# An attention and expert-layer kernel on one core: list scatters in pairs, gathers spread over the units, stored weights in longer runs

## The chip, the core and the metric

The kernel runs on one core of a Trainium2 chip. The metric is the device time of one execution in microseconds (us). Its engines are TensorE (PE, the matmuls; PEld is the loading of its weights), VectorE (DVE), ScalarE (ACT), GpSimd (POOL) and SyncE (SP), which mostly issues transfers. Each works through its own queue in order, and they wait for each other by semaphores.

## What is computed

Attention without softmax, followed by a layer of eight experts of which every token uses at most one:

```python
# 8 batches, 2496 rows, u and v 256 wide, z 64 wide
scores = np.matmul(z, z.transpose(0, 2, 1)) / S
attn = np.maximum(scores, 0.0) ** 2
x = (u * np.matmul(attn, v)).reshape(19968, 256)

out = x.copy()
xc = x[x @ w_skip > 0]                   # the others stay as they are
e_idx = np.argmax(xc @ w_gate, axis=1)   # one of 8 experts
gate_w = softmax of xc @ w_gate, at e_idx
for e in range(8):
    h = np.maximum(xc[e_idx == e] @ w1[e], 0.0)     # 256 -> 1024
    y[e_idx == e] = gate_w[...] * (h @ w2[e])       # 1024 -> 256
out[do_compute] = xc + y
```

All of it is fp32. The kernel splits every operand in a high part and a low part (`ah`/`al`, `vh`/`vl`, `zh`/`zl`, `hh`/`hl`) and multiplies high with high, high with low and low with high.

## The kernel before

**Attention.** A batch has five chunks of queries: four of 512 and a short one of 448, so 40 chunks. A chunk is done in ten steps; a step takes 256 keys. `weights` makes a step's two key tiles: six score matmuls into PSUM (L251), relu and square on ACT (L297, L298), the high part by a cast (`high`, ACT at L304 or DVE at L306, as `on_act` says), the low part by a subtraction on DVE (`low`, L309). Then 24 matmuls (L333) add the step's product with `v` to four accumulators. `stage` prepares a step two steps (`LA`) ahead of its matmuls. At a chunk's last step `part` reads the accumulators (L361, L363), `mul` multiplies by `u` (L366), and later `turn_rows` (L370) and `store` (L379) write the rows to the buffer `xr` in DRAM and to `out`.

The scores are symmetric. For the pairs (chunk c, key block j) in `PAIRS`, chunk c stores its squared scores, transposed (`keep`, L268), and chunk j reads them back instead of computing them (`recall`, L287). The stores are put into a list; `put_some` (L663) issues at most four of them per step, on SP, not before the second step after. `ahead` issues the reads five steps ahead. Where the key block is the short chunk's (j = 4), a pair of key tiles is stored in 14 transfers of 64 KB, of 32 elements (128 bytes) in a run; else in 4 of 256 KB with runs of 128 elements (512 bytes). The short chunk recalls four of its ten steps, 4 to 7, and casts (ACT) and subtracts (DVE) 2 × 448 = 896 columns in one operation each.

**Routing.** After every second chunk, `routing` works out to which expert each of about 1000 tokens goes: `gates` two steps later, `logits` three, `route` and `counts` four, and `place` six. `place` has eight small matmuls, five small DVE operations (L472 to L477) that end in `dest`, the slot of each token in its expert's list, and eight indirect transfers on POOL (L480), each of which scatters the 8-byte entries of 128 tokens into `lst` in DRAM. The order of all this is the order of the code: `after` and `todo` say at which step each function runs, and the instructions stand in the engines' queues as the functions issue them. The last routing runs in the first unit of expert 0 (`end_routes`); the one before it, after chunk 38, in steps of chunk 39.

**Experts.** An expert's list is worked through in units of two tiles of 128 tokens. Three units (`NFIX`) are always done; a switch then picks an arm with as many further tiles as the list has (units of two or three). Before a unit its rows must be gathered (`fetch`, L528, one indirect transfer on POOL per tile), transposed on PE (`turn_pe`, L546) and split (ACT L548, DVE L549). The unit itself is 48 matmuls for the hidden layer (L575), relu and split (L580, L581), 48 matmuls back (L594), the combination (L623) and two scatters of the results (L624) on POOL. `fills` says which side work is issued after which part of a unit, by slot numbers 0 to 7: gathers, transposes, and the pieces of the next expert's weights (`load_w`), whose low parts POOL subtracts (L151 and L157, for the experts from 2 on).

Rows sit in tiles `xgf` (four: two per parity of the expert, its first two units) and `xgu` (four, in turn). In the fixed unit i of an expert after the first, slot 0 gathers unit i + 2, and in unit 0 slot 1 gathers the next expert's units 0 and 1 together (`next_rows`). An arm gathers two units ahead where there are so many.

## Time and profile before

| | us |
|---|---|
| runs | 1937.83, 1925.1, 1917.16; median 1925.1 |
| profiled execution | 1936.81, its span 1935.0 |
| mean granted clock of TensorE | 0.983 of full speed |
| busy: PE, DVE, ACT, POOL | 1836.9, 1212.5, 1107.0, 418.9 |
| list scatters (L480) | 160, 1.134 each |
| gathers (L528) | 84, about 1.03 each |
| recalled short chunk tiles | 32 casts of 0.938, 32 subtractions of 1.082 |

Attention fills the span to about 1400 us, and the experts the rest. A window's row gives its length, then the busy time and the number of instructions of each engine in it, then PEclk (the clock that TensorE was granted, as a share of full speed), the share of the DMA engines' time in use and GB/s. A group's row gives the busy time, the mean of one instruction in ns, and behind the bar the idle time before them and what ended it. A row of the timeline gives start, length, engine, line, operation, and in brackets the idle time before and its end; "remote" there means that the record of what ended it is not in the trace.

### The profile page before, as it was taken

What the parts mean: (1) busy time and instruction counts of PE and PEld (TensorE: products, weight loads), DVE (VectorE), ACT (ScalarE), POOL (GpSimd) and SP (SyncE); (2) the same over time, 40 slices, a digit from 0 to 9 for tenths busy, and PEclk for the clock granted to TensorE, in tenths of its full rate; (3) what the DMA queues carried; (4) which work ended last, traced back from release to release, by engine and by line L of the source; (5) the groups of instructions that cost most, each with busy time, mean ns of one, the idle gap of its engine ahead of it and who ended that gap; (6) DMA issues with size and microseconds to landing.
All of it is one profiled execution on the core that took longest, in us unless ns stands there. A gap on an engine that the chain in (4) does not pass through costs nothing.

```text
span 1935.0 us, 40227 instructions
## 1 busy us (share of the span) xinstructions
PE 1836.9 (95%) x15928; PEld 1595.0 (82%) x15928; DVE 1212.5 (63%) x1998; ACT 1107.0 (57%) x1350; POOL 418.9 (22%) x417
## 2 busy tenths in 40 slices
PE   8999999899999999999999999999889989999998
PEld 6888778777877877787878788777789989998998
DVE  6777777677777777777777777767643333333333
ACT  8766676667667666756775775666423223322321
POOL 0111110110110111011021011101334345534532
PEclk9999999999999999999999999999989999999999
DMA  5584677377557747775783777468542223212211
GB/s 175 122 172 115 157 185 163 81 192 168 129 123 192 148 101 183 173 155 109 174 172 88 182 173 157 107 144 174 115 112 64 63 85 96 71 56 83 76 36 34
DMA packets 468400, 246.98 MB, mean 128 GB/s; under 512 B 321571, under 2 KB 410917, under 8 KB 468080
## 3 DMA queue, kind: packets, MB, share of 16 engines
q1 hardware_dynamic: 454656, 221.61, 49.4%
q0 software_dynamic: 13136, 21.42, 3.8%
q8 instruction: 142, 2.33, 0.5%
q14 instruction: 178, 1.46, 0.3%
q10 hardware_dynamic: 288, 0.17, 0.0%
HBM read 134.79 MB, written 108.95 MB: 126 GB/s over the span
## 4 chain that ended last, share of the span: by engine, by line
PE 63%; DMA 9%; DVE 8%; ACT 7%; issue 6%; SPq 4%; another core or an unknown queue 2%; POOL 1%; POOLq 0%; DVEq 0%; ACTq 0%
PE acc L333 36%; PE psh L575 9%; PE y L594 9%; PE ps L251 7%; DMA out<-o,idt 4%; ACT r L297 2%; ACT r L298 2%; DVE al L309 2%; SPq L379 2%; ACT ah L304 2%; DMA kept<-rt 2%; SPq L663 1%; DVE rt L268 1%; PE psm L401 1%
## 5 line engine op out<-in xcount | busy, mean ns | idle before, releaser
L333 PE MATMUL acc<-ah,vh 64*128 64x512 f32 (+1 forms) x3120 | 739.3, 391 | 41.0 <-ACT xrow L361 17.8
L333 PE MATMUL acc<-ah,vl 64*128 64x512 f32 (+1 forms) x3120 | 719.9, 389 | 0.2
L309 DVE TENSOR_TENSOR al<-r,ah 128x1024 fp32r<-128x1024 f32 (+1 forms) x400 | 475.7, 1194 | 199.1 <-ACT ah L304 179.6
L333 PE MATMUL acc<-al,vh 64*128 64x512 f32 (+1 forms) x3120 | 566.2, 387 | 2.0 <-DVE al L309 1.2
L333 PEld LDWEIGHTS acc<-ah,vh 64*128 64x128 f32 x3120 | 426.5, 186 | 121.9 <-ACT xrow L361 21.8
L333 PEld LDWEIGHTS acc<-ah,vl 64*128 64x128 f32 x3120 | 427.3, 187 | 49.7 <-issue 2.0
L297 ACT ACTIVATE r<-ps 128x1024 f32<-128x1024 f32 (+1 forms) x292 | 294.4, 1008 | 259.3 <-PE ps L251 178.3
L480 POOL DMA_INDIRECT lst<-pair,dest x160 | 181.4, 1134 | 1180.8 <-DVE dest L477 1119.5
L333 PEld LDWEIGHTS acc<-al,vh 64*128 64x128 f32 x3120 | 364.6, 186 | 58.5 <-DVE al L309 6.0
L298 ACT ACTIVATE r<-r 128x1024 f32<-128x1024 f32 (+1 forms) x292 | 304.6, 1043 | 9.2
L304 ACT CAST ah<-r 128x1024 fp32r<-128x1024 f32 (+1 forms) x265 | 271.5, 1036 | 32.9 <-DMA r<-kept 13.6
L580 ACT ACTIVATE hh<-psh 128x512 fp32r<-128x512 f32 (+1 forms) x172 | 99.6, 585 | 316.2 <-PE psh L575 251.1
L594 PE MATMUL y<-w2t,hh 128*128 128x256 f32 x1328 | 249.9, 289 | 0.8 <-issue 0.8
L575 PE MATMUL psh<-xt,w1h 128*128 128x256 f32 (+1 forms) x1280 | 234.5, 286 | 14.4 <-issue 10.2
L581 DVE SCALAR_TENSOR_TENSOR hl<-psh,hh 128x512 fp32r<-128x512 f32 (+1 forms) x172 | 113.8, 672 | 164.4 <-ACT hh L580 138.7
L575 PEld LDWEIGHTS psh<-xt,w1h 128*128 128x128 f32 x1280 | 199.3, 191 | 16.0 <-issue 11.4
L594 PEld LDWEIGHTS y<-w2t,hh 128*128 128x128 f32 x1328 | 210.9, 195 | 1.7 <-issue 1.7
L594 PE MATMUL y<-w2t,hl 128*128 128x256 f32 x664 | 190.0, 286 | 1.8 <-issue 1.8
L575 PE MATMUL psh<-xt,w1l 128*128 128x256 f32 (+1 forms) x640 | 182.1, 285 | 0.0
L251 PE MATMUL ps<-zh 64*128 64x512 f32 (+1 forms) x584 | 145.3, 407 | 14.7 <-ACT r L297 6.8
L306 DVE CAST ah<-r 128x1024 fp32r<-128x1024 f32 (+1 forms) x135 | 90.3, 669 | 86.6 <-ACT r L298 73.3
L251 PE MATMUL ps<-zl,zh 64*128 64x512 f32 (+1 forms) x584 | 141.3, 393 | 0.0
(169 smaller groups left out, 1725.2 us busy)
## 6 DMA issues: line engine op xcount, KB each, us to landing
kept<-rt SPq DMA_DIRECT2D x152, 256.0 KB
r<-kept SPq DMA_DIRECT2D x304, 128.0 KB
raw<-in_v SPq DMA_DIRECT2D x80, 256.0 KB
ut<-in_uT SPq DMA_DIRECT2D x32, 512.0 KB
xr<-xrow SPq DMA_DIRECT2D x128, 128.0 KB
out<-xrow SPq DMA_DIRECT2D x128, 128.0 KB
raw<-in_w SPq DMA_DIRECT2D x64, 256.0 KB
kept<-rt SPq DMA_DIRECT2D x224, 64.0 KB
```

Of the source, the lines that this page charges most:

```text
L251: nc.tensor.matmul(to, k[h, o : o + P], queries(q, h, n), start=(m == 0), stop=(m == 2))
L297: nc.scalar.activation(r[:, :, :n], ps[:, :, :n], AF.Relu, scale=isc)
L298: nc.scalar.activation(r[:, :, :n], r[:, :, :n], AF.Square)
L304: nc.scalar.copy(ah[:, :, :n], r[:, :, :n])
L306: nc.vector.tensor_copy(ah[:, :, :n], r[:, :, :n])
L309: nc.vector.tensor_sub(al[:, :, :n], r[:, :, :n], f32(ah[:, :, :n]))
L333: nc.tensor.matmul(acc[t][:, :n], w[h, x, dd], a[h, x, :n], start=(first and t not in halves[:m]), stop=(last and t not in halves[m + 1 :]),)
L480: put = nc.gpsimd.indirect_dma_start(out=lst, out_offset=bass.IndirectOffsetOnAxis(ap=dest[:, t : t + 1], axis=0), in_=pair[:, t, :], in_o ...
L575: nc.tensor.matmul(ps[:, j * W : (j + 1) * W], wt[:, a, o : o + P], x[:, d, :W], start=(m == 0), stop=(m == 5),)
L580: nc.scalar.activation(hh[:, : G * W], ps[:, : G * W], AF.Relu)
L581: nc.vector.scalar_tensor_tensor(hl[:, : G * W], ps[:, : G * W], 0.0, f32(hh[:, : G * W]), op0=ALU.max, op1=ALU.subtract)
L594: nc.tensor.matmul(ys[t], h[:, tt], w2t[f][:, k, :], start=(f == 0 and m == 0 and t % 2 == 0), stop=(f == NF - 1 and m == 2), skip_group_c ...
```

## The change

*The list scatters.* `place` ends with the sums `df`. A new function `put_in(t0, t1)` computes `dest` for the tiles t0 to t1 and issues their scatters. It runs for two tiles at the steps 6, 8, 10 and 12 after the routing's chunk; for the routing after chunk 38 at 6, 7, 8 and 9; and in `end_routes` for all four tiles at once.

*The gathers.* There are six `xgf` tiles, for all three fixed units of two experts, and `xgu` holds the units of the arms. In fixed unit i of an expert e after the first, slot 0 gathers unit i + 3 and slot 3 gathers unit i of expert e + 1. All six tiles of the arm's first three units are thus reserved ahead of the switch: always three, whether or not the arm has them; in the arm, further units are gathered three ahead. That makes 96 gathers of 128 rows rather than 84. Expert 0's units and the loads of the lists' ids are moved accordingly.

*The short chunk's stored weights.* All stores are 4 transfers of 256 KB in runs of 512 bytes, whatever the key block, and all reads take the full 512 columns, so the short chunk's columns come back in another order. The cast and the subtraction undo that in three pieces: for each of the two key tiles 3 × 128 columns, and 64 columns of both together.

```diff
             dst = kept[c, j].rearrange("(m i) k -> i m k", i=32)
             for a in range(4):
-                h = slice(32 * a, 32 * a + 32)
-                if j < NQ - 1:
-                    puts.append((step[0], dst[:, :, a * P : a * P + P], t[h]))
-                else:
-                    for k in range(4 if a < 2 else 3):
-                        o = k * P + 32 * a
-                        puts.append((step[0], dst[:, :, o : o + 32], t[h, :, 32 * k : 32 * k + 32]))
+                puts.append((step[0], dst[:, :, a * P : a * P + P], t[32 * a : 32 * a + 32]))
...
+        views = [[x[:, :, :n] for x in (r, ah, al)]]
+        if old and n < QC:
+            b3 = 3 * P
+            views = [
+                [r.rearrange("p x (a k e) -> p x k a e", a=4, k=4)[:, x, :3]]
+                + [t[:, x, :b3].rearrange("p (k a e) -> p k a e", a=4, k=3) for t in (ah, al)]
+                for x in range(2)
+            ] + [
+                [r.rearrange("p x (a k e) -> p x k a e", a=4, k=4)[:, :, 3, : (n - b3) // 32, :]]
+                + [t[:, :, b3:n].rearrange("p x (a e) -> p x a e", e=32) for t in (ah, al)]
+            ]
         def high():
-            if on_act(ci, p):
-                nc.scalar.copy(ah[:, :, :n], r[:, :, :n])
-            else:
-                nc.vector.tensor_copy(ah[:, :, :n], r[:, :, :n])
+            for r_, h_, _ in views:
+                (nc.scalar.copy if on_act(ci, p) else nc.vector.tensor_copy)(h_, r_)
         def low():
-            nc.vector.tensor_sub(al[:, :, :n], r[:, :, :n], f32(ah[:, :, :n]))
+            for r_, h_, l_ in views:
+                nc.vector.tensor_sub(l_, r_, f32(h_))
...
             nc.vector.tensor_reduce(df, ds_, axis=AX.X, op=ALU.add)
-            nc.vector.tensor_scalar_add(dest[:, :K], df, float(BIG))
-            puts = []
-            for t in range(K):
+            put_sums.append(df)
+        puts, put_sums = [], []
+        def put_in(t0, t1):
+            df = put_sums[0]
+            nc.vector.tensor_scalar_add(dest[:, t0:t1], df[:, t0:t1], float(BIG))
+            for t in range(t0, t1):
                 put = nc.gpsimd.indirect_dma_start(
...
+                    last = ci + 2 > NC - 1
+                    for t in range(0, 4 * len(new), 2):
+                        k = 6 + (t // 2 if last else t)
+                        after.append((lambda put_in=put_in, t=t: put_in(t, t + 2), k))
...
-        return xgs["f"][2 * (e % 2) + i] if e and i < 2 else xgs["u"][i % 4]
+        return xgs["f"][NFIX * (e % 2) + i] if i < NFIX else xgs["u"][i % 4]
...
             if e:
-                add(fills, (0, lambda: fetch(ids_of(e, i + 2), pair(e, i + 2))))
-                add(fills, (3, lambda: turn_pe(pair(e, i + 1), turned(e, i + 1))))
-                if more and i == 0:
-                    add(fills, (1, lambda: next_rows(e + 1)))
-                if more and i == 1:
-                    add(fills, (5, lambda: turn_pe(pair(e + 1, 0), turned(e + 1, 0))))
+                add(fills, (0, rows(e, i + 3)), (3, lambda: turn_pe(pair(e, i + 1), turned(e, i + 1))))
+                if e == 1 and i == 0:
+                    fills[0].insert(0, rows(1, 2))
+                if more:
+                    add(fills, (3, rows(e + 1, i)))
...
+            elif i == 1:
+                add(fills, (3, lambda: turn_pe(pair(0, 2), turned(0, 2))), (5, rows(0, 3)), (5, rows(0, 4)))
...
             else:
-                    add(fills, (0, lambda: next_rows(1)), (4, lambda: turn_pe(pair(0, 3), turned(0, 3))),
-                        (7, lambda: turn_pe(pair(1, 0), turned(1, 0))))
+                add(fills, (0, rows(1, 0)), (4, lambda: turn_pe(pair(0, 3), turned(0, 3))),
+                    (4, rows(0, 5)), (4, rows(1, 1)), (6, lambda: load_ids(idts[2], 2, 2 * NSTAT)))
+            if more and i == 2:
+                add(fills, (7, lambda: turn_pe(pair(e + 1, 0), turned(e + 1, 0))))
...
-                    if len(after) > 1 or after[0] == 3:
-                        m = 2 if len(after) > 1 else 1
-                        add(fills, (0, lambda: fetch(ids_of(e, i + 2, m), pair(e, i + 2), m)))
+                    if i + 3 < end:
+                        add(fills, (0, rows(e, i + 3)))
```

The order on VectorE after the third routing's `place`, in the first chunks of the second batch, before (L309 is `low`, L306 a cast of `high`, L361 to L366 the reading of the accumulators and the multiply):

```order
L474 TENSOR_TENSOR ds__2789<-psm,ds__2789 128x64
L475 TENSOR_TENSOR ds__2789<-ds__2789,hot 128x64
L476 TENSOR_REDUCE df<-ds__2789 128x8
L477 TENSOR_SCALAR dest<-df 128x8
L309 TENSOR_TENSOR al<-r,ah 128x1024
```

and in the changed kernel, whose line numbers are its own (L314 is `low`, L490 `dest`, L310 a cast, L366 to L371 the accumulators and the multiply):

```order
L490 TENSOR_SCALAR dest<-df 128x2
L314 TENSOR_TENSOR al<-r,ah 128x1024
L268 STREAM_TRANSPOSE rt<-r 128x16x32 x2
L310 CAST ah<-r 128x1024
L314 TENSOR_TENSOR al<-r,ah 128x1024
L490 TENSOR_SCALAR dest<-df 128x2
L314 TENSOR_TENSOR al<-r,ah 128x1024
L268 STREAM_TRANSPOSE rt<-r 128x16x32 x2
L366 COPY xrow<-acc 128x512
L368 TENSOR_TENSOR xrow<-acc,xrow 128x512 x2
L314 TENSOR_TENSOR al<-r,ah 128x1024
L371 TENSOR_TENSOR ut<-xrow,ut 128x1024
```

Before, one `dest` of 128 x 8 stands directly behind the reduction. Now the first of four does, the second stands two steps on, and the third follows the last row shown, directly behind the chunk's multiply.

POOL in the fixed units of expert 2, first before, where `idt_142` holds expert 2's ids and `idt_143` expert 3's:

```order
L528 DMA xgu<-xr,idt_142 128x256 x2
L528 DMA xgf<-xr,idt_143 128x256 x4
L151 TENSOR_TENSOR w1l<-raw,w1h 128x512 x3
L624 DMA out<-o,idt_142 19968x256 x2
L528 DMA xgu<-xr,idt_142 128x256 x2
L151 TENSOR_TENSOR w1l<-raw,w1h 128x512
L157 TENSOR_TENSOR w2t<-raw,w2t 128x256 x4
L624 DMA out<-o,idt_142 19968x256 x2
L858 TENSOR_LOAD arm
L528 DMA xgu<-xr,idt_142 128x256 x2
L157 TENSOR_TENSOR w2t<-raw,w2t 128x256 x4
```

and in the changed kernel (L540 gathers, L636 scatters the results):

```order
L540 DMA xgu<-xr,idt_142 128x256 x2
L151 TENSOR_TENSOR w1l<-raw,w1h 128x512
L540 DMA xgf<-xr,idt_143 128x256 x2
L151 TENSOR_TENSOR w1l<-raw,w1h 128x512 x2
L636 DMA out<-o,idt_142 19968x256 x2
L540 DMA xgu<-xr,idt_142 128x256 x2
L151 TENSOR_TENSOR w1l<-raw,w1h 128x512
L540 DMA xgf<-xr,idt_143 128x256 x2
L157 TENSOR_TENSOR w2t<-raw,w2t 128x256 x4
L636 DMA out<-o,idt_142 19968x256 x2
L875 TENSOR_LOAD arm
L540 DMA xgu<-xr,idt_142 128x256 x2
```

Six gathers in a row have become two pairs with a subtraction between them, and each unit has four gathers; the `xgu` rows of a unit are those of the unit three later, no longer two.

SP in the first batch's chunk 2 to 4, before, with the stores of pair (2, 4), whose key block is the short chunk's (`kept_138`):

```order
L663 DMA kept_138<-rt 32x16x32 x8
L287 DMA r<-kept_137 32x2x512 x4
L663 DMA kept_138<-rt 32x16x32 x4
L95 DMA raw<-in_v 128x512
L663 DMA kept_138<-rt 32x16x32 x2
L287 DMA r<-kept_137 32x2x512 x4
```

and in the changed kernel:

```order
L675 DMA kept_138<-rt 32x16x128 x4
L280 DMA r<-kept_137 32x2x512 x4
L95 DMA raw<-in_v 128x512
L280 DMA r<-kept_137 32x2x512 x4
L384 DMA xr<-xrow 32x16x64 x4
```

Fourteen issues between the reads have become four ahead of them.

More of the change, by code (lines that the diff above doesn't have):

```diff
@@ L490, in place @@
                 puts.append(put)
-        return gates, logits, route, counts, place
+        return gates, logits, route, counts, place, put_in
     def count(name, rows64=True):
@@ L764, in attn_moe @@
                 if ci % 2 == 0:
-                    gates, logits, route, counts, place = routing(new)
+                    gates, logits, route, counts, place, put_in = routing(new)
                     after = [(gates, 2), (rows0, 2), (logits, 3), (rows1, 3), (route, 4), (counts, 4),
                              (store, 4), (store, 5), (place, 6)]
+                    last = ci + 2 > NC - 1
+                    for t in range(0, 4 * len(new), 2):
+                        k = 6 + (t // 2 if last else t)
+                        after.append((lambda put_in=put_in, t=t: put_in(t, t + 2), k))
                     new = []
@@ L771, in attn_moe @@
             else:
-                gates, logits, route, counts, place = routing(new, False)
+                gates, logits, route, counts, place, put_in = routing(new, False)
         for f in todo.pop(s, []):
@@ L775, in attn_moe @@
         put_some()
-    row_tiles("f", 4)
+    row_tiles("f", NFIX)
+    row_tiles("u", 4)
     ps_s_own.close()
@@ L821, in add, with rows @@
             fills.setdefault(k, []).append(f)
-    def next_rows(e):
-        for i in range(2):
-            fetch(ids_of(e, i), pair(e, i))
+    def rows(e, i):
+        return lambda: fetch(ids_of(e, i), pair(e, i))
     for e in range(E):
@@ L843, in attn_moe @@
                     (5, store), (5, store), (6, end_routes))
-            else:
-                if i == 1:
-                    add(fills, (3, lambda: turn_pe(pair(0, 2), turned(0, 2))),
-                        (6, lambda: [fetch(ids_of(0, k), pair(0, k)) for k in (3, 4)]))
-                    add(fills, *zip((1, 3, 5), wq[:3]))
-                else:
-                    add(fills, (0, lambda: next_rows(1)), (4, lambda: turn_pe(pair(0, 3), turned(0, 3))),
-                        (7, lambda: turn_pe(pair(1, 0), turned(1, 0))))
-                    add(fills, *zip((1, 2, 3, 5, 6), wq[3:]))
-            if i == (0 if e else 2) and e + 2 < E:
-                add(fills, (6, lambda: load_ids(idts[e + 2], e + 2, 2 * NSTAT)))
+            elif i == 1:
+                add(fills, (3, lambda: turn_pe(pair(0, 2), turned(0, 2))), (5, rows(0, 3)), (5, rows(0, 4)))
+                add(fills, *zip((1, 3, 5), wq[:3]))
+            else:
+                add(fills, (0, rows(1, 0)), (4, lambda: turn_pe(pair(0, 3), turned(0, 3))),
+                    (4, rows(0, 5)), (4, rows(1, 1)), (6, lambda: load_ids(idts[2], 2, 2 * NSTAT)))
+                add(fills, *zip((1, 2, 3, 5, 6), wq[3:]))
+            if more and i == 2:
+                add(fills, (7, lambda: turn_pe(pair(e + 1, 0), turned(e + 1, 0))))
             if i == NFIX - 1:
@@ L873, in attn_moe @@
                     unit(0, 2, ids_of(0, i), [xg[:, 0, :], xg[:, 1, :]], xts[0])
+            end = NFIX + (sum(ws) + 1) // 2
             for j, w in enumerate(ws):
```

12 lines of the change are left out of this document (7 added, 5 removed).

## The prediction, made before the changed kernel ran

> **What bounds the kernel now.** I read the page first, then windows around every run of list scatters, then the waits of TensorE behind the attention.
>
> ```profile
> span 1935.0 us, 40227 instructions
> PE 1836.9 (95%) x15928; PEld 1595.0 (82%) x15928; DVE 1212.5 (63%) x1998; ACT 1107.0 (57%) x1350; POOL 418.9 (22%) x417
> ```
>
> TensorE (PE) is the bound: 1935.0 − 1836.9 = 98.1 us without a matmul in flight. The change removes no matmul, so it can win only two things: part of that idle time, and busy time that was stretched because the granted clock (PEclk) fell. The question is where both sit.
>
> The list scatters (L480) go out in runs of eight in 18 of the 21 places where they are issued. I took three windows about each of these 18 starts: its first 6 us, the next 12 us, and the 18 us before. Columns: length, busy us and instructions per engine, PEclk, DMA share, GB/s. The sum over the 18 first-6-us windows:
>
> ```profile
> sum 108.00, PE 108.00 PEld 95.73 DVE 80.51 ACT 72.05 POOL 87.80; mean PE 6.00 PEld 5.32 DVE 4.47 ACT 4.00 POOL 4.88
> ```
>
> Three of the 18 next-12-us windows, and the sum of the 18:
>
> ```profile
> 347.80:359.80 12.00, 6.71 (x46) 5.17 (x43) 7.64 (x10) 6.63 (x8) 4.03 (x5) 0.82 0.01 0
> ...
> 1039.90:1051.90 12.00, 8.38 (x54) 6.81 (x52) 8.97 (x12) 5.64 (x6) 4.36 (x5) 0.72 0.02 2
> ...
> 1181.60:1193.60 12.00, 10.79 (x75) 7.99 (x75) 7.53 (x10) 5.31 (x7) 4.51 (x5) 0.86 0.74 138
> ...
> sum 216.00, PE 182.53 PEld 140.46 DVE 146.01 ACT 122.60 POOL 78.00; mean PE 10.14 PEld 7.80 DVE 8.11 ACT 6.81 POOL 4.33
> ```
>
> One of the windows before, and the sum of the 18:
>
> ```profile
> 323.80:341.80 18.00, 17.62 (x195) 16.56 (x193) 14.46 (x39) 9.57 (x13) 0.00 (x0) 1.00 0.68 176
> sum 324.00, PE 314.70 PEld 255.73 DVE 258.06 ACT 221.95 POOL 0.14; mean PE 17.48 PEld 14.21 DVE 14.34 ACT 12.33 POOL 0.01
> ```
>
> The 12 us from the start of two runs of only four scatters:
>
> ```profile
> 73.70:85.70 12.00, 12.00 (x105) 10.69 (x103) 8.82 (x11) 10.00 (x12) 5.08 (x4) 1.00 0.72 167
> 1414.40:1426.40 12.00, 12.00 (x104) 12.00 (x103) 6.00 (x14) 3.89 (x7) 6.95 (x8) 1.00 0.61 96
> ```
>
> While scatters one to four go out nothing happens (108.00 of 108.00); from about the fifth on TensorE loses 216.00 − 182.53 = 33.5 us. In the quiet windows it loses 9.3 in 324, which would be 6.2 in 216, so 27.3 us belong to the scatters. The clock falls in 7 of the 18 windows, to between 0.72 and 0.86; summing (1 − PEclk) × 12 over them gives 15.4 us more. Two runs of four cost nothing: 12.00 of 12.00 each. The worst place, as a timeline:
>
> ```profile
> 341.82 1.17 POOL L480 DMA_INDIRECT lst<-pair,dest  x1 [49.77 <-DVE dest L477]
> ...
> 351.60 0.97 POOL L480 DMA_INDIRECT lst<-pair,dest  x1 [0.30 <-issue]
> 353.63 1.02 ACT L297 ACTIVATE r<-ps 128x1024 f32<-128x1024 f32 x1 [4.73 <-remote]
> 353.73 0.62 DVE L361 COPY xrow<-acc 128x448 f32<-128x448 f32 x1 [2.67 <-remote]
> 356.22 0.80 PE L333 MATMUL acc<-ah,vh 64*128 64x512 f32 x2 [4.97 <-ACT xrow L361]
> ```
>
> These are the first and the eighth scatter on GpSimd (POOL), then ScalarE (ACT) and VectorE (DVE), which had waited 4.73 and 2.67 us for a signal that the trace doesn't hold ("remote") and start again 1.1 us after the eighth scatter's end, and TensorE after them. Transfers hardly ran there (0.01 in row 347.80), so crowded DMA engines are not the cause; a backlog of scatters fits, since runs of four make no gap.
>
> In the expert part, one row of TensorE's waits (us in all, times, longest) and three windows:
>
> ```profile
> PE pst L546 <- DMA xgu<-xr,idt: 11.9, 6, 2.7
> 1564.00:1578.00 14.00, 9.12 (x62) 8.78 (x62) 2.30 (x5) 1.04 (x3) 7.74 (x9) 0.88 0.42 138
> 1757.00:1773.00 16.00, 11.49 (x64) 11.14 (x63) 3.03 (x6) 2.13 (x6) 7.98 (x10) 0.79 0.42 122
> 1818.00:1830.00 12.00, 9.32 (x67) 9.14 (x66) 2.04 (x5) 1.66 (x4) 7.29 (x10) 0.86 0.19 55
> ```
>
> and on the timeline:
>
> ```profile
> 1501.27 1.05 POOL L528 DMA_INDIRECT xgu<-xr,idt  x1 [0.30 <-issue]
> 1504.24 0.41 PE L546 MATMUL pst<-ident,xgu 128*128 128x128 f32 x2 [1.99 <-DMA xgu<-xr,idt]
> ```
>
> TensorE waits 11.9 us, in six places, for gathered rows that it is about to transpose: POOL issues them at 1501.27, TensorE has them at 1504.24. The clock loss beside such waits is 14 × 0.12 + 16 × 0.21 + 12 × 0.14 = 6.7 us. The rest of TensorE's idle time in this part, at the switches between units, is not touched.
>
> **Part A, scatters two at a time.** Each routing now issues two scatters at its steps 6, 8, 10 and 12 (a step is 30 matmuls, at the 12.00 / 105 = 0.114 us of row 73.70 that is 3.4 us), so a pair has some 7 us to itself.
>
> ```profile
> L477 DVE TENSOR_SCALAR dest<-df 128x8 int32<-128x8 f32 x19 | 3.3, 172 | 0.6
> L480 POOL DMA_INDIRECT lst<-pair,dest x160 | 181.4, 1134 | 1180.8 <-DVE dest L477 1119.5 <-issue 41.8 <-DVE cnt L498 18.9
> ```
>
> Added: three small `dest` operations for each of 18 full routings and one more for the four-tile one, 55 × 0.172 = 9.5 us of VectorE in all, half a microsecond in any one chunk. VectorE is busy 14.46 of 18 us at the densest place shown; the work that hides it is the matmuls of two steps lookahead. Without that cover it would cost 9.5 us. Only POOL waits for `dest`, and behind the scatters on POOL there is one small memset for the next routing; nothing else is queued there during attention. At step 10 `dest` stands behind the chunk's multiply, that is after the accumulators have been read, so no accumulator is released later. A pair occupies POOL for 2 × (1.134 + 0.30) = 2.9 us of its 7, so the backlog that takes five scatters to build is never reached. To be won: at most 27.3 + 15.4 = 42.7 us, at least nothing if pairs meet a cost of their own (rivals). I take 36, about 85%: residue of 0.35 us per routing. The last routing has its four pairs one step apart, which is close to the run of eight that it had; I give it nothing either way.
>
> [...] The row first: 1181.60:1193.60 shows 0.86 although it lost only 12.00 − 10.79 = 1.2 us in all. [...]
>
> **Part B, gathers a unit ahead.** In the fixed units of an expert (three units of 96 matmuls, at the 12.00 / 104 = 0.115 us of row 1414.40 that is 11.1 us each, 33.2 us) POOL had ten gathers and six scatters and now has twelve and six, always three tiles of two: the last may be rows that the expert's arm never uses, twelve gathers more in all.
>
> ```profile
> L528 POOL DMA_INDIRECT xgu<-xr,idt x50 | 51.6, 1032 | 50.8 <-issue 25.6 <-DMA xgu<-xr,idt 9.9 <-DVE xt L549 8.2
> L157 POOL TENSOR_TENSOR w2t<-raw,w2t 128x256 fp32r<-128x256 f32 x48 | 33.8, 737 | 0.1
> L151 POOL TENSOR_TENSOR w1l<-raw,w1h 128x512 fp32r<-128x512 f32 x24 | 30.6, 1298 | 0.4
> ```
>
> POOL's bill for these units: 18 × (1.03 + 0.30 before the next, as at 1501.27) = 23.9, the scatters of the results priced like gathers, plus 4 × 1.298 + 8 × 0.737 = 11.1, together 35.0 against 33.2 us. It ends 1.8 us late and catches up in the arm, which has 22 us and no weights. A gather is now due two units after its issue, so 1.8 us of lateness is covered; without that cover it would be 7 × 1.8 = 13 us. All six waits should go, with their clock: 11.9 + 6.7 = 18.6; I take 16. Expert 0's third unit gains between 0 and 10 us from a shorter run of POOL transfers:
>
> ```profile
> 1423.00:1450.00 27.00, 21.80 (x154) 20.40 (x153) 9.73 (x21) 7.35 (x18) 12.23 (x13) 0.81 0.63 161
> ```
>
> (27.00 − 21.80 + 0.19 × 27 = 10.3). The run is still ten long, so I take 0 and keep 10 for the low end.
>
> **Part C, the short chunk's weights.** They leave in 64 stores of 256 KB and not 224 of 64 KB, and are read back at full width. The cast and the subtraction behind them (32 of each) go in three pieces of 384, 384 and 128 columns.
>
> ```profile
> kept<-rt SPq DMA_DIRECT2D x224, 64.0 KB
> ...
> L304 ACT CAST ah<-r 128x896 fp32r<-128x896 f32 x32 | 29.7, 938 | 13.0 <-PE acc L333 9.5 <-DVE al L309 3.5
> L119 ACT CAST vh<-raw 128x512 fp32r<-128x512 f32 x80 | 49.3, 616 | 17.4 <-DMA raw<-in_v 17.2
> L156 ACT CAST w2t<-raw 128x256 fp32r<-128x256 f32 x64 | 22.8, 407 | 11.0 <-DMA raw<-in_w 9.2 <-issue 1.8
> L309 DVE TENSOR_TENSOR al<-r,ah 128x896 fp32r<-128x896 f32 x80 | 86.3, 1082 | 5.7 <-ACT ah L304 0.6 <-DVE ah L306 0.5 <-DMA xr<-xrow 0.3
> L549 DVE TENSOR_TENSOR xt<-pst,xt 128x512 fp32r<-128x512 f32 x38 | 25.9, 683 | 11.9 <-ACT xt L548 8.9 <-issue 2.9
> L549 DVE TENSOR_TENSOR xt<-pst,xt 128x256 fp32r<-128x256 f32 x10 | 4.2, 424 | 29.6 <-ACT xt L548 29.6
> ```
>
> On the line through 256 and 512 columns, ACT needs 2 × 0.51 + 0.30 = 1.32 us for 0.94 (+0.39), DVE 2 × 0.55 + 0.29 = 1.40 for 1.08 (+0.32): 12.4 and 10.1 us over the kernel, in four successive steps of eight short chunks. Window 323.80:341.80 is such a chunk: ACT has 8.4 us free of 18 and DVE 3.5, against 1.6 and 1.3 added. I count 0; uncovered it is 22.5 us. The 160 DMA issues fewer on SP (SyncE), and transfers in longer runs, were waited for by nobody in the rows above: also 0, a few us of gain at best.
>
> **Sum.** 36 + 16 + 0 = 52 us off the profiled execution, 1936.8 → 1885. That run was the slowest of three, 11.7 us above their median; what varies between runs is likely these very waits, so for the median I take half of that off the gain: 1925.1 − 46 = **1879**.
>
> **Rivals.** *The number of scatters matters, not their run.* Then A gives nothing and B stands: 1925 − 16 = 1909. For it: they still number 160, beside the same engines. Against: the four-scatter rows without a gap. [...]
>
> *Only a part is won:* A brings a third or a half of its 42.7 (14 to 21, that is 15 to 22 less than the 36), because gaps move with the step-10 pair to the change of chunks, or B brings half since POOL stays full (8 less). Both together leave 46 − 23 = 23: about 1902.
>
> *Slower: every start of a run has its price.* If the gap is the landing of the last scatter of a group and not the backlog, 27.3 / 18 = 1.5 us come at the end of each of 72 groups rather than of 18: 72 × 1.5 = 109, less 42.7 and 16, is +50, about 1975. It decides from (42.7 + 16) / 72 = 0.8 us for each pair, and is over 1% from 1.1. Against: the runs of four, also with an end, without a gap.
>
> *No effect:* gaps come from where step 6 lies in the chunk and POOL stays saturated: 1925.
>
> **Chances.** Forecast 0.60; part 0.15; only B 0.13; no effect 0.04; slower 0.08. The measurement tells about 1% from no change, 19 us. Faster by more: 0.60 + 0.15 = 0.75. Within: 0.13 + 0.04 = 0.17. Slower: 0.08. Range: down to 1925 − 42.7 − 18.6, with a part of the 10 of expert 0, about 1858; up past B alone, 1912. That leaves out slower, no effect, and edges, some 0.2.
>
> **What would show it.** In the windows of 12 us behind each routing's step 6: TensorE at 11.5 or more, PEclk 1.00, and pairs of scatters 7 us apart. No row `pst` waiting for `xgu` over 1 us. Short-chunk casts as three operations of about 0.5, 0.5 and 0.3 us, with no new wait for them by TensorE. It is wrong if gaps with "remote" stand behind pairs, if ACT or DVE becomes what `acc` matmuls wait for in the short chunk, or if POOL's gathers slip past their unit.

## The result, and the profile after

The changed kernel takes 1863.96 us (median of 4 runs, 1862.88 to 1865.33) where the kernel before takes 1927.63 (4 runs, 1917.16 to 1937.83): a ratio of 0.967, 95% interval 0.9616 to 0.9724. That is 64 us, where 46 were forecast; 1864 lies in the range of 1858 to 1912. On another chip, below, the same two kernels stand much closer.

The top of the page after:

```profile
span 1863.6 us, 40331 instructions
## 1 busy us (share of the span) xinstructions
PE 1803.3 (97%) x15928; PEld 1589.9 (85%) x15928; DVE 1218.0 (65%) x2120; ACT 1113.3 (60%) x1414; POOL 438.3 (24%) x429
```

The matmuls are the same 15928, and still PE's busy time fell by 33.6 us: the same work ran at a higher clock (0.983 of full speed on average before, 0.995 after) and closer together. To see where the 71.4 us between the two profiled spans came from, I cut both at the last attention matmul. Windows of the kernel before:

```profile
0.00:1394.60 1394.60, 1335.44 (x11825) 1097.80 (x11825) 1020.83 (x1648) 951.75 (x1042) 187.31 (x179) 0.99 0.65 150
1394.60:1935.00 540.40, 501.42 (x4103) 497.19 (x4103) 191.71 (x350) 155.25 (x308) 231.56 (x239) 0.97 0.25 70
```

and of the kernel after:

```profile
0.00:1349.00 1349.00, 1308.76 (x11825) 1098.15 (x11825) 1027.05 (x1769) 958.28 (x1107) 192.50 (x177) 1.00 0.63 158
1349.00:1863.60 514.60, 494.52 (x4103) 491.76 (x4103) 190.95 (x351) 154.99 (x308) 245.83 (x252) 0.98 0.28 76
```

Attention gave 1394.6 − 1349.0 = 45.6 us: 18.9 of idle time (59.2 to 40.2) and 26.7 of busy time. The clock's own records, summed over attention, account for 17.1 of the 26.7 (17.1 lost before, nothing after). The experts gave 540.4 − 514.6 = 25.8 us, 18.9 of them idle time.

Behind the routings, the 12 us windows that the prediction used, now after: the fourth and the sixteenth routing, and the sum of the 18.

```profile
341.90:353.90 12.00, 11.77 (x105) 9.75 (x103) 11.30 (x17) 9.16 (x10) 5.19 (x5) 1.00 0.01 2
...
1145.80:1157.80 12.00, 12.00 (x118) 10.76 (x116) 8.72 (x12) 6.84 (x9) 3.20 (x4) 1.00 0.31 91
...
sum 216.00, PE 209.75 PEld 177.49 DVE 180.17 ACT 146.90 POOL 79.51; mean PE 11.65 PEld 9.86 DVE 10.01 ACT 8.16 POOL 4.42
```

6.25 us are lost in 216, where 33.5 were; that is what the quiet windows of before lost (9.3 in 324, which is 6.2 in 216). PEclk is 1.00 in all 18. At the worst place of before, the timeline after reads:

```profile
340.77 1.33 POOL L492 DMA_INDIRECT lst<-pair,dest  x1 [2.00 <-DVE dest L490]
...
342.26 1.03 ACT L290 ACTIVATE r<-ps 128x1024 f32<-128x1024 f32 x1 [0.50 <-PE ps L251]
342.41 1.75 POOL L492 DMA_INDIRECT lst<-pair,dest  x1 [0.30 <-issue]
343.32 1.06 ACT L291 ACTIVATE r<-r 128x1024 f32<-128x1024 f32 x1
343.83 0.62 DVE L366 COPY xrow<-acc 128x448 f32<-128x448 f32 x1
```

Beside the second pair ScalarE waits 0.50 us for a matmul with a name, and no longer 4.73 for "remote".

TensorE's waits in the expert part, first before (three rows), then after:

```profile
PE pst L546 <- DMA xgu<-xr,idt: 11.9, 6, 2.7
PE psh L575 <- issue: 10.2, 5, 2.4
PE psh L575 <- DVE xt L549: 4.2, 1, 4.2
```

```profile
PE y L606 <- issue: 3.6, 5, 1.1
PE pst L558 <- issue: 3.0, 4, 1.1
PE psh L587 <- issue: 2.6, 2, 2.1
PE psh L587 <- DVE xt L561: 1.7, 1, 1.7
```

No wait for gathered rows is left, and 7.6 us of the "issue" wait ahead of the hidden layer went too.

The pieces of the short chunk, and the small `dest`, as groups after:

```profile
L314 DVE TENSOR_TENSOR al<-r,ah 128x384 fp32r<-128x384 f32 x64 | 32.2, 544 | 0.2
L310 ACT CAST ah<-r 128x384 fp32r<-128x384 f32 x64 | 29.5, 509 | 11.1 <-PE acc L338 9.7 <-issue 1.4
L490 DVE TENSOR_SCALAR dest<-df 128x2 int32<-128x2 f32 x78 | 12.5, 160 | 0.7
L310 ACT CAST ah<-r 128x128 fp32r<-128x128 f32 x32 | 9.4, 295 | 0.0
L314 DVE TENSOR_TENSOR al<-r,ah 128x128 fp32r<-128x128 f32 x32 | 9.2, 286 | 0.0
```

### The profile page after: what moved, and what is told of

It is laid out like the page before. It is cut to its first block, busy times and chain, and to the rows that moved or that the text cites. A ratio compares the mean times of both kernels' runs of the same rounds, so it can differ in the third digit from the quotient of the medians.

```text
span 1863.6 us, 40331 instructions
## 1 busy us (share of the span) xinstructions
PE 1803.3 (97%) x15928; PEld 1589.9 (85%) x15928; DVE 1218.0 (65%) x2120; ACT 1113.3 (60%) x1414; POOL 438.3 (24%) x429
## 3 DMA queue, kind: packets, MB, share of 16 engines
q8 instruction: 143, 2.34, 0.6%
## 4 chain that ended last, share of the span: by engine, by line
PE 70%; DVE 9%; ACT 7%; DMA 6%; issue 4%; SPq 3%; POOL 0%; DVEq 0%; POOLq 0%; ACTq 0%
PE acc L338 38%; PE y L606 11%; PE psh L587 11%; PE ps L251 7%; DVE al L314 2%; ACT r L290 2%; ACT ah L310 2%; ACT r L291 2%; SPq L384 2%; DMA out<-o,idt 2%; DVE rt L268 1%; DMA r<-kept 1%; DMA kept<-rt 1%; DVE xrow L368 1%; PE psm L406 1%
## 5 line engine op out<-in xcount | busy, mean ns | idle before, releaser
L314 DVE TENSOR_TENSOR al<-r,ah 128x1024 fp32r<-128x1024 f32 (+3 forms) x464 | 480.4, 1050 | 188.3 <-ACT ah L310 173.2
L338 PEld LDWEIGHTS acc<-ah,vh 64*128 64x128 f32 x3120 | 431.7, 185 | 89.4 <-DVE xrow L368 14.5
L338 PEld LDWEIGHTS acc<-ah,vl 64*128 64x128 f32 x3120 | 432.0, 185 | 46.7
L492 POOL DMA_INDIRECT lst<-pair,dest x160 | 189.0, 1181 | 1141.8 <-DVE dest L490 1101.0
L310 ACT CAST ah<-r 128x1024 fp32r<-128x1024 f32 (+1 forms) x329 | 277.3, 872 | 28.2 <-PE acc L338 11.6
L251 PE MATMUL ps<-zh,zl 64*128 64x512 f32 (+1 forms) x584 | 143.2, 390 | 0.0
```

The lines of the kernel that those rows point to most:

```text
L251: nc.tensor.matmul(to, k[h, o : o + P], queries(q, h, n), start=(m == 0), stop=(m == 2))
L310: (nc.scalar.copy if on_act(ci, p) else nc.vector.tensor_copy)(h_, r_)
L314: nc.vector.tensor_sub(l_, r_, f32(h_))
L338: nc.tensor.matmul(acc[t][:, :n], w[h, x, dd], a[h, x, :n], start=(first and t not in halves[:m]), stop=(last and t not in halves[m + 1 :]),)
L492: put = nc.gpsimd.indirect_dma_start(out=lst, out_offset=bass.IndirectOffsetOnAxis(ap=dest[:, t : t + 1], axis=0), in_=pair[:, t, :], in_o ...
```

## The experiments

Theory: a run of scatters holds TensorE up once it is some five long, and the expert part waits for rows that were gathered too late. Rivals: it is the number of scatters, or the end of each group, that costs; and the parts may overlap or hide each other's loss.

The runs fall into four groups, each on a chip of its own. This matters more than expected: the unchanged kernel before takes 1904.2 us on the first of these chips, 1863.7 on the second, 1902.7 on the third and 1866.4 on the fourth, beside 1927.6 in the result's run, whose chip is not known. So kernels are compared only within a chip.

### Each part alone

The scatters alone, the gathers alone and the stores alone are the hunks of the diff, put one at a time into the kernel before. The fourth kernel has the scatters in fours:

```diff
-                    for t in range(0, 4 * len(new), 2):
+                    for t in range(0, 4 * len(new), 4):
                         k = 6 + (t // 2 if last else t)
-                        after.append((lambda put_in=put_in, t=t: put_in(t, t + 2), k))
+                        after.append((lambda put_in=put_in, t=t: put_in(t, t + 4), k))
```

> The kernel before with only the list scatters in pairs. In the two traces the stretch from the first full routing to the last one but one shrank by 46 us (138.4 to 1345.8 before, 138.6 to 1300.0 after). Theory (a run of scatters is what costs): about 46 us faster than before, some 1881, and the windows behind a routing's step 6 without TensorE's gaps. Rival (their number costs): no difference, 1927. Rival (each start of a group costs): slower than before.

> The kernel before with only the gathers moved. From the last routing to the end the two traces differ by 26 us (549.8 and 523.9 us), 19 of them idle time of TensorE. Theory: about 26 us faster, some 1901, with the 11.9 us of waits for gathered rows gone and most of the 10.2 us that stood as issue in front of the hidden layer's matmuls. By the prediction's term it would be 16, some 1911. If the expert part gained only because the attention part no longer ended in scatters, nothing.

> The kernel before with only the short chunk's stored weights changed. After, TensorE waits 7.3 us in 8 places for ScalarE's cast in front of the attention matmuls, before 2.8 in 3 places. Theory: the three-piece cast costs about 4 to 5 us, some 1932. Rival (longer runs of the stores pay for it, or it is hidden, as predicted): 1927 or a few us less.

> The kernel before with the scatters in two runs of four, at steps 6 and 10, instead of one of eight. Theory (a run costs from about the fifth scatter): like the pairs alone, about 1881 to 1885, since the two runs of four in the kernel before showed no gap. Rival (each group's end has a price of 1.5 us): 18 ends more, about 27 us slower than the run of eights is now, 1950. Rival (number): 1927.

Against 1904.2 us of before on this chip:

| | median us | ratio, 95% interval |
|---|---|---|
| scatters in pairs | 1880.3 | 0.9874 (0.9831 to 0.9918) |
| scatters in fours | 1884.8 | 0.9881 (0.9831 to 0.9932) |
| gathers | 1884.7 | 0.9899 (0.9863 to 0.9935) |
| stores | 1895.9 | 0.9963 (0.9935 to 0.9990) |

The 18 windows of 24 us from each routing's first scatter show the attention part by itself (432 − PE is the loss). The kernel with only the gathers moved still has the runs of eight:

```profile
sum 432.00, PE 408.64 PEld 343.95 DVE 319.65 ACT 282.34 POOL 166.11; mean PE 22.70 PEld 19.11 DVE 17.76 ACT 15.69 POOL 9.23
```

in pairs alone:

```profile
sum 432.00, PE 426.35 PEld 376.93 DVE 348.69 ACT 300.06 POOL 172.62; mean PE 23.69 PEld 20.94 DVE 19.37 ACT 16.67 POOL 9.59
```

in fours:

```profile
sum 432.00, PE 423.73 PEld 367.33 DVE 337.77 ACT 295.34 POOL 178.56; mean PE 23.54 PEld 20.41 DVE 18.77 ACT 16.41 POOL 9.92
```

and in eights with the new stores:

```profile
sum 432.00, PE 416.52 PEld 353.71 DVE 327.72 ACT 296.30 POOL 171.88; mean PE 23.14 PEld 19.65 DVE 18.21 ACT 16.46 POOL 9.55
```

Eights lose 23.4 us, fours 8.3, pairs 5.7, with 160 scatters each time. So it is the run's length; the rivals of number and of the group's end fall (fours have twice the ends of eights and lose a third). The pairs gained 24 us and not 46, mainly because this chip's eights cost less. The attention part of these two traces, eights and pairs, differs by 25.8 us (1370.3 and 1344.5), and in the 18 windows eights lose 23.4 us here and 34.2 in the result's run of before:

```profile
sum 432.00, PE 397.84 PEld 326.33 DVE 305.85 ACT 267.42 POOL 165.80; mean PE 22.10 PEld 18.13 DVE 16.99 ACT 14.86 POOL 9.21
```

The gathers alone gained 19.5, somewhat under the 26 expected; their waits for rows are gone in that trace, and stand unchanged at 11.7 us where only the scatters were changed:

```profile
PE pst L553 <- DMA xgu<-xr,idt: 11.7, 6, 3.1
PE psh L582 <- issue: 6.3, 4, 2.0
```

The stores alone were expected to cost 4 to 5 us. They gained 8: that expectation was wrong, and so was its reason, since the wait for ScalarE's cast, 7.3 us after and 2.8 before, is 6.5 us with pairs alone, without any three-piece cast, and only 3.7 with the stores alone:

```profile
PE acc L333 <- ACT ah L304: 6.5, 7, 0.9
...
PE acc L338 <- ACT ah L310: 3.7, 4, 0.9
```

What the stores gained lies behind the routings too, 8 of their windows' 23.4 us, most plainly at the fourth routing, in a short chunk. First eights with the old stores, then with the new:

```profile
338.80:362.80 24.00, 20.53 (x188) 17.97 (x186) 18.39 (x24) 16.85 (x18) 9.14 (x9) 1.00 0.12 38
```

```profile
339.70:363.70 24.00, 23.77 (x215) 22.46 (x213) 21.03 (x28) 18.48 (x20) 10.59 (x9) 1.00 0.13 38
```

Why they soften the runs of eight there isn't settled: it could be the shorter queue of stores, or the pieces' other timing. These were not tried apart.

### What the runs do to TensorE's signals

The traces hold the times of semaphore updates. TensorE's signalling matmuls, 1343 in before and 1330 in the changed kernel, all update one semaphore; the delay below goes from the end of the signalling matmul to the next update of that semaphore, as a median over the 18 routings, by the time since the routing's first scatter. Single values can be wrong where a record is missing, medians less so. The entries move with the edges of the bins: in the first row a shift by half a microsecond takes the one at 2-4 us to 0.40 or 0.71, and the one at 4-6 us, with six matmuls, to 0.80 or 2.06. Worked out from the traces:

```
us since the first scatter     0-2   2-4   4-6   6-8   8-10  10-12 12-14
before (result's run)          0.02  0.60  1.31  2.34  1.55  0.61  0.01
gathers alone (eights)         0.02  0.25  0.76  1.21  0.74  0.79  0.01
stores alone (eights)          0.02  0.13  0.27  0.94  0.22  0.71  0.01
before (third chip)            0.02  0.04  0.63  0.57  0.02  0.77  0.01
fours alone                    0.02  0.13  0.72  0.01  0.01  0.02  0.01
pairs, every step (third)      0.02  0.07  0.25  0.69  0.02  0.41  0.01
pairs alone                    0.02  0.02  0.02  0.01  0.01  0.01  0.01
changed kernel (result's run)  0.02  0.02  0.02  0.01  0.01  0.01  0.01
changed kernel (second chip)   0.02  0.01  0.02  0.01  0.01  0.01  0.01
```

Outside the scatters the median delay is 0.01 to 0.02 us (0.02 over the 599 signalling matmuls of before's attention that are further than 25 us behind a run's start). In the result's run and in eights on the first chip it is longest 6 to 8 us after the first scatter (2.34, 1.21 and 0.94), behind the fifth and sixth, and it is back at 0.01 once the run has landed. The worst place of before in detail (times in us): the signals of matmuls that ended at 343.87, 344.28 and 344.99 arrived at 344.02, 344.78 and 346.25. Matmuls that ended at 348.12, 348.93, 349.15, 349.94 and 351.24 carry five more, and the next five updates stand at 353.61, 353.70, 353.74, 353.84 and 353.91. The eighth scatter landed from 353.53 to 353.70. This is what "remote" at 353.63 and 353.73 was: TensorE had finished 2.7 to 5.5 us before, with the five matched in order, and nobody knew. The update is in the trace after all; what the view doesn't find is a matmul that ended shortly before it. VectorE's updates were not late there: its operations that ended at 349.12 and 350.45 have theirs 0.01 us later. The scatters themselves didn't queue up: the fifth to eighth were issued at 347.53, 348.81, 350.27 and 351.60 and landed at 349.5, 350.9, 352.3 and 353.6, two us later each time. So the backlog is one of TensorE's signals and not, as the prediction had it, of scatters.

TensorE's matmuls are held up as well, with nothing that the profile shows them to wait for ("issue"). The row of such waits in attention, before and after:

```profile
PE acc L333 <- issue: 9.6, 16, 2.2
...
PE acc L338 <- issue: 0.4, 2, 0.3
```

Two limits. The traces with the delay lack records: 1312 updates stand for 1343 signalling matmuls in before, and 1256 for 1330 in the changed kernel. Where none is missing in a routing and they can be matched in order (8 of 18 routings in before, 7 in the changed kernel), single delays reach 5.5 us with eights and 0.4 with pairs, so the reading holds. And the traces of the second and fourth chip, below, which show no delay, lack none of these updates. So it may be that the recording of the profile has a part in the delay; this was not tried.

### All parts together, the number doubled, and a further version

The changed kernel once more; the same without the new stores (the hunks on `keep`, `recall` and `weights` undone); one in which every pair is followed by the same pair into a second list that nobody reads; and a further version.

```diff
+            for t in range(t0, t1 if t1 - t0 == 2 else t0):
+                put = nc.gpsimd.indirect_dma_start(
+                    out=lst2,
```

The further version, without the new stores:

```diff
+                        if last and t == 6:
+                            tail = lambda put_in=put_in: put_in(6, 8)
+                        else:
+                            after.append((lambda put_in=put_in, t=t: put_in(t, t + 2), 6 + t))
...
-                add(fills, (0, gates), (1, logits), (2, route), (3, rows0), (4, counts), (5, rows1),
+                add(fills, (0, gates), (1, logits), (1, tail), (2, route), (3, rows0), (4, counts), (5, rows1),
...
-(5, rows(0, 3)), (5, rows(0, 4)))
+(5, rows(0, 3)))
...
-                add(fills, (0, rows(1, 0)), (4, lambda: turn_pe(pair(0, 3), turned(0, 3))),
-                    (4, rows(0, 5)), (4, rows(1, 1)), (6, lambda: load_ids(idts[2], 2, 2 * NSTAT)))
+                add(fills, (0, rows(0, 4)), (3, rows(1, 0)), (4, lambda: turn_pe(pair(0, 3), turned(0, 3))),
+                    (7, rows(0, 5)), (7, rows(1, 1)), (6, lambda: load_ids(idts[2], 2, 2 * NSTAT)))
```

> The changed kernel once more, beside the others of this job on one chip. In the job before, on another chip, its parts alone gained 24 (scatters), 19 (gathers) and 8 us (stores). Theory: the gains of scatters and stores overlap, since the stores alone emptied the same windows behind a routing, so all three together gain about 24 + 19 = 43 to 48 us against the kernel before on the same chip. Rival: they add up, 52 us or more.

> The changed kernel with the short chunk's stored weights as before. Theory (with the scatters in pairs nothing is left for the stores to gain, and the three-piece casts cost little): within 4 us of the changed kernel, either way. Rival: the stores gain their 8 us here too, and this one is 8 us slower. Rival from the changed kernel's waits: 4 to 5 us faster without the three-piece casts.

> The changed kernel with every pair of scatters followed by the same pair into a second list that nobody reads: 312 list scatters rather than 160, in runs of four, 5.7 of 6.9 us of GpSimd. Theory (a run costs from about the fifth scatter, with a pause it costs nothing): within 5 us of the changed kernel. Rival (number): twice the loss that eights had on that chip, 25 to 40 us slower.

> The changed kernel with the stored weights as before, with the last routing's pairs at steps 6, 8, 10 and in expert 0's first unit instead of four successive steps, and with expert 0's gathers apart (units 3, 4 and expert 1's first at three places, the other two at the end of its third unit). Theory: the last routing's 2.9 us of idle time and 3.4 of clock go, and of the 10 us lost about expert 0's third unit some; 6 to 14 us faster than the changed kernel. Rival (those losses are not the runs' doing): no difference.

This was the second chip, where before takes 1863.7 us:

| | median us (lowest to highest) | ratio to before, 95% interval |
|---|---|---|
| changed kernel | 1852.9 (1850.3 to 1859.2) | 0.9936 (0.9910 to 0.9961) |
| without the new stores | 1848.1 (1844.1 to 1850.9) | 0.9920 (0.9892 to 0.9948) |
| scatters twice | 1867.4 (1864.4 to 1875.2) | 1.0022 (1.0004 to 1.0040) |
| further version | 1850.0 (1846.6 to 1852.0) | 0.9923 (0.9896 to 0.9950) |

The whole change is worth 10.8 us here, not 43 or 52. The delay is at 0.01 to 0.02 us through all scatters in each of these traces. So neither reading of the sum can be told from this chip: what the pairs were to remove seems not to be there.

Behind the 18 routings no run of eight was traced on this chip. But the changed kernel itself has a longer one: about expert 0's third unit, GpSimd issues twelve indirect transfers (gathers and scatters of results) without a pause in the result's run, and sixteen here. The same 20 us of the same kernel, first in the result's run, then on this chip:

```profile
1380.00:1400.00 20.00, 13.35 (x81) 12.29 (x81) 8.22 (x18) 6.52 (x16) 10.06 (x10) 0.74 0.60 158
...
1380.00:1400.00 20.00, 19.44 (x166) 18.95 (x166) 12.52 (x26) 10.13 (x22) 13.31 (x13) 1.00 0.77 212
```

81 matmuls went out in the one and 166 in the other. In the result's run TensorE's matmuls there go out singly, 0.72 us or twice that apart, and ScalarE waits for a late signal until 1.7 us after the end of the run's last transfer on GpSimd:

```profile
1388.06 0.27 PE L558 MATMUL pst<-ident,xgu 128*128 128x128 f32 x1 [0.44 <-issue]
1388.78 0.32 PE L558 MATMUL pst<-ident,xgu 128*128 128x128 f32 x1 [0.45 <-issue]
1390.20 0.37 PE L558 MATMUL pst<-ident,xgu 128*128 128x128 f32 x1 [1.11 <-issue]
1394.52 0.60 ACT L592 ACTIVATE hh<-psh 128x512 fp32r<-128x512 f32 x1 [8.96 <-remote]
```

So a long run held TensorE up on the one chip (13.35 of 20 us busy) and not on the other (19.44), with the kernel the same.

The new stores cost some 5 us in the presence of the other two parts; the two kernels' own ranges overlap by 0.6 us, and there is no interval for that pair. The further version brought nothing: 1850.0 against 1848.1 of the version that it builds on, so its theory falls on this chip, where the loss about expert 0's third unit that it was to win isn't there. On one with the delay it wasn't tried.

Twice the scatters cost 14.5 us, so the theory (within 5 us) missed the total; but the cost isn't where the rival has it. Its windows in attention lose what pairs lose, 6.0 us:

```profile
sum 432.00, PE 425.95 PEld 364.92 DVE 349.61 ACT 302.51 POOL 319.26; mean PE 23.66 PEld 20.27 DVE 19.42 ACT 16.81 POOL 17.74
```

From the last attention matmul on it takes 519.5 us, the changed kernel 503.1 on this chip; there TensorE waits 1.3 us for gathered rows (`xgf`), none in the changed kernel on this chip, and 5.5 us for "issue" ahead of the hidden layer, 3.9 in the changed kernel; where the rest of the 16.4 us comes from isn't shown.

### The kernel before on another chip, pairs closer together, gathers in fours

The pairs one step apart and the gathers in one run are one line each:

```diff
-                        k = 6 + (t // 2 if last else t)
+                        k = 6 + t // 2
```

```diff
-                    add(fills, (3, rows(e + 1, i)))
+                    add(fills, (0, rows(e + 1, i)))
```

> The kernel before, unchanged, for a profile on this chip. In the traces so far TensorE's signals (its semaphore updates) reached the waiting engines 0.01 us after a matmul's end outside the scatters, but behind the sixth to eighth scatter of a run with a median lag of 1.2 to 2.3 us on two chips, and 0.01 on the third, where the whole change gained only 11 us. Theory: where this profile shows the lag, TensorE loses 20 to 45 us in the 18 routings' windows; where it doesn't, it loses no more there than the changed kernel does. Rival: gaps without a lag.

> The changed kernel with the pairs one step apart instead of two (GpSimd then issues for 2.9 of 3.4 us). Theory (the lag grows while scatters go out without a pause): on a chip with the lag 5 to 25 us slower than pairs two steps apart, about what six in a row cost; on a chip without it no difference. Rival (any pause is enough): no difference on either.

> The changed kernel with all four gathers of a fixed unit in its slot 0, in one run, instead of two and two. Theory (what helped the expert part is that rows are gathered a unit earlier than needed, not how they are spread): within 4 us of the changed kernel. Rival (runs on GpSimd hold up TensorE here too): 5 us slower or more on a chip with the lag.

On this third chip before takes 1902.7 us (7 runs); the pairs at every step take 1865.1 (ratio 0.9786, 0.9750 to 0.9822) and the gathers in fours 1874.6 (0.9844, 0.9810 to 0.9878). The profile of before on this chip shows the delay (table above) and loses 17.8 us behind the routings:

```profile
sum 432.00, PE 414.17 PEld 351.87 DVE 328.52 ACT 287.67 POOL 170.19; mean PE 23.01 PEld 19.55 DVE 18.25 ACT 15.98 POOL 9.46
```

A little under the 20 expected, and the smallest loss of the three traces with eights and the old stores that show the delay. In these traces eights lose wherever the delay is, and the size of both goes together only roughly: the largest median is 2.34 us with 34.2 us lost, 1.21 with 23.4, 0.94 with 15.5 (the stores alone), and 0.77 with 17.8. The median alone doesn't set the loss: fours lost only 8.3 us with 0.72.

Pairs at every step lose 9.0 us in the same windows:

```profile
sum 432.00, PE 422.96 PEld 359.35 DVE 344.54 ACT 299.87 POOL 169.65; mean PE 23.50 PEld 19.96 DVE 19.14 ACT 16.66 POOL 9.43
```

The delay is there (0.69 us), but the loss is only some 3 us above pairs two steps apart, not the 5 to 25 expected. The kernel with the gathers in fours has such pairs, and on this same chip it loses 6.0:

```profile
sum 432.00, PE 425.96 PEld 367.94 DVE 349.08 ACT 303.05 POOL 174.14; mean PE 23.66 PEld 20.44 DVE 19.39 ACT 16.84 POOL 9.67
```

That short pauses keep the delay within what the two steps of lookahead cover is a likely reading, and not shown.

The gathers in one run of four are 9.5 us slower than the kernel beside them, whose runs don't overlap with theirs (1868.9 to 1875.2, and 1861.0 to 1866.5); the two differ by the scatters too, but the other one's, at every step, are the costlier ones. So spreading seems to matter, and the theory that only the lead does looks wrong; the changed kernel itself, with which the theory compares, didn't run on this chip. The lead does its own part: in this trace as well TensorE waits for no gathered row. Where the 9.5 us are isn't shown: the two profiled runs differ by 2.4 us (1868.9 and 1866.5), their expert parts by 3.6 (520.4 and 516.8).

### The number doubled, once more

> Again the changed kernel with every pair of scatters followed by the same pair into a list that nobody reads (312 list scatters, runs of four, 5.7 of 6.9 us of GpSimd). On the chip without the lag it was 14 us slower than the changed kernel. Theory (where TensorE's signals lag, the lag is a matter of the run's length, four is short enough): the 18 routings' windows as empty as in the changed kernel, the lag back at 0.01 us between the runs, and in all 10 to 20 us slower than the changed kernel's 1864. Rival (number): the windows lose as much as the eights did, 20 to 45 us, and it is no faster than the kernel before.

This chip turned out to be one without the delay again (0.01 to 0.02 us throughout). Before takes 1866.4 us, the doubled scatters 1869.7 (ratio 1.0017, 1.0003 to 1.0031), and the windows lose 6.1 us:

```profile
sum 432.00, PE 425.90 PEld 369.66 DVE 349.93 ACT 302.88 POOL 319.01; mean PE 23.66 PEld 20.54 DVE 19.44 ACT 16.83 POOL 17.72
```

So the doubled number was tried only where there is no delay to see, and its total can't be set against the 1864 of another chip; on a chip with the delay, only the fours speak against the number.

## Why the prediction was right, and where its steps were off

**Where the time sits** was read rightly. The windows behind the routings went from 33.5 us lost to 6.25, the level of the quiet windows of before (6.2), with the clock at 1.00 in all of them; this was the larger part, and the gathers' waits were the second. (There are 19 runs of eight, not 18; the nineteenth, at 1385.16, is the last routing but one, which the prediction takes apart as the last. Nothing rests on it but half a microsecond of `dest`.)

**That the number fits is in part luck.** 46 us were forecast and 64 came, and the forecast knew nothing of chips: on the second one the same change is worth 10.8 us, less than the 13 that the slow end of the range allows.

**Part A was sized at 36 us and gave 45.6** in the profiled runs, above what it was said to be able to give at most, 42.7. The step that failed is that bound: it counted idle time (27.3) and lost clock (15.4) in windows of 12 us. The clock's records over the whole of attention show 17.1, and a third term was left out: of the 26.7 us by which busy time fell, 9.6 are not the clock. A busy stretch can hold matmuls that go out further apart. The rows show it by their counts, here one window at full clock before, and its like after:

```profile
837.70:849.70 12.00, 10.47 (x85) 7.60 (x83) 7.26 (x10) 5.14 (x7) 4.30 (x5) 1.00 0.69 119
...
812.10:824.10 12.00, 12.00 (x118) 10.76 (x116) 8.69 (x12) 6.76 (x10) 3.27 (x4) 1.00 0.34 89
```

In the eleven windows with PEclk 1.00 before, 1023 matmuls took 122.34 us, 0.120 each; in the same eleven after, 1165 took 128.98, 0.111 each. That is about 9 us on 1023. The idle term was smaller than counted, 18.9: the windows gave back 33.5 − 6.25 = 27.2, so outside these windows TensorE's idle time grew by 8.3. The attention part contains the new stores too; alone on the first chip they gained 8 us in the same windows, so not all of the 45.6 need be the pairs' doing.

**The mechanism of A was half right.** The run's length decides, as the fours show (8.3 us lost, and 23.4 with eights), and not number or ends. But it wasn't a backlog of scatters; TensorE's signals are late while the scatters go out, and its matmuls go out further apart. "While scatters one to four go out nothing happens" holds for TensorE's busy time alone: the median delay was 0.60 and 1.31 us already from 2 to 6 us after the first scatter. And about its longer run the same kernel lost 0.6 us in 20 on the second chip, so the run's length decides only where the delay is.

**Part B was sized at 16 us and gave 25.8.** The 11.9 us of waits for rows went to nothing, as forecast. The step that failed is the sentence that the rest of the idle time at the switches between units is not touched: the "issue" wait fell from 10.2 to 2.6 us. It reads as a consequence of the late rows: four of its five places stand 4.8 to 6.7 us behind a wait for rows, as this one behind the wait at 1504.24 that the prediction shows, and with the gathers alone moved it was gone too:

```profile
1509.88 0.47 PE L575 MATMUL psh<-xt,w1h 128*128 128x256 f32 x2 [2.36 <-issue]
```

GpSimd's 35.0 us of work in 33.2 was no obstacle. Expert 0's third unit was left at no gain, and the trace after still shows its loss: 6.7 us of idle time and 5.2 of clock in the row 1380.00:1400.00 above.

**Part C was priced rightly and valued wrongly.** The pieces take 509, 295, 544 and 286 ns where 510, 300, 550 and 290 were drawn from other shapes, and the added 22 us are not seen as a wait for the three pieces. But its value isn't zero: 8 us of gain while eights are there, some 5 us of loss without them.

**The median.** Half of the 11.7 us between the profiled run and the median was taken off, because what varies between runs was thought to be these waits. The changed kernel's runs spread over 2.5 us and those of before over 20.7, which agrees; the sum that the half was taken off was too small by the two terms above: 52, where the profiled runs differ by 71.5.

**The clock, and the scatters' own time.** The clock fell beside a small loss too: PEclk was 0.86 in the window 1181.60:1193.60, which lost 1.2 us. All of the 17.1 us in attention came back. The scatters' time on GpSimd goes with VectorE's work: the 25 list scatters of before that have no VectorE operation beside them take 0.97 to 0.98 us, and the other 135 take 1.16 on average and up to 2.01. The reason isn't shown. That TensorE pays for it isn't shown either: with the scatters doubled the windows in attention lost 6.0 and 6.1 us, on chips without the delay, and where TensorE was held up its own signals and matmuls were late.

## What to carry to other kernels

When idle time stands behind "remote" or an unknown releaser, compare the end of the last matmul before it with the update of its semaphore: a late signal looks like a slow engine (ScalarE's 4.73 us of "remote" here). Issue indirect transfers on GpSimd a few at a time with pauses between, which alone gained 23.9 us on the first chip, where the delay was, and showed no cost on the second, where pairs and moved gathers together were 15.6 us faster than before, and fetch their data a unit of work earlier than needed: with the gathers moved TensorE's 11.9 us of waits for rows were gone. Measure such a change on more than one chip: the whole of this one was worth 64 us in the result's run and 10.8 on the second chip.

## What the runs showed of the hardware that was not expected

- TensorE's semaphore updates arrived 0.01 to 0.02 us after a matmul outside runs of indirect scatters (median), and, 6 to 8 us after the first scatter of a run of eight, 2.34 us after it in the result's run and 1.21 and 0.94 on the first chip; the largest median on the third is 0.77. On the second and fourth chip no trace showed it, and in a run of sixteen transfers on the second TensorE was busy for 19.44 of 20 us. Why chips differ, what the signals wait for, and whether the recording of the profile takes part, stays open.
- The same kernel's time differed from chip to chip: before takes 1863.7 to 1904.2 us on the four chips and 1927.6 in the result's run, the changed kernel 1852.9 on the second chip and 1864.0 in the result's run.
- Attention's matmuls counted as busy took 9.6 us more in all, beyond the lost clock, in before, with such delays, than in the changed kernel; about a run of twelve transfers of the latter they went out 0.72 us or twice that apart.
- In before a list scatter takes 0.97 to 0.98 us with VectorE idle beside it (25 of 160), and 1.16 on average and up to 2.01 with VectorE at work.
